# Paired block loads, weights in ten parts, and idle products in a recurrent attention and mixture-of-experts kernel

## The chip, the cores and the metric

The kernel runs on one core of a Trainium2 chip. The metric is the device time of one execution in microseconds. Before the change the median of three runs was 463.25 us (462.76 to 464.66). About 0.5% of that, 2.3 us, can be told from no change.

## The reference

Two parts follow each other. The first is a gated linear recurrence for 4 batch rows and 8 heads, 768 time steps, head size 48:

```python
for t in range(S):
    state = alpha[:, :, t, :, None] * state + np.einsum('bhd,bhe->bhde', k[:, :, t], v[:, :, t])
    y[:, :, t] = np.einsum('bhd,bhde->bhe', q[:, :, t], state)
```

Its result, seen as 3072 rows of 384 numbers, goes through a mixture of eight experts. Each row picks the expert with the largest logit:

```python
logits = x @ w_gate
expert_idx = np.argmax(logits, axis=1)
...
h = np.maximum(x_sorted[lo:hi] @ w1[e], 0.0)
y_sorted[lo:hi] = h @ w2[e]
...
return gate_w[:, None] * y
```

All data are 32-bit floats. An expert's w1 is 384 x 1024, its w2 1024 x 384.

## The kernel before

**Blocks.** Time is cut into 6 chunks of 128 steps. A block s is one chunk of one batch row with all 8 heads: chunk s // 4, batch row s % 4, so 24 blocks, chunk by chunk. Within a block the recurrence is done with matrix products; between chunks a state per batch row is carried on.

**What happens to a block.** Its parts, by the names of the functions: `load` brings alpha, k, q and v (192 KB each, in pieces of 48 numbers, 192 bytes) from memory, on the queue of SyncE. `logs` takes the logarithm of alpha on ScalarE. `cums` makes the running sum over time with a product by a triangular matrix on TensorE (tile `cum`, one PSUM bank), and its exponentials `cp` and `icp` on ScalarE. It also sends one row of each to the tiles `dec`, by small transfers on SyncE's queue. `operands` multiplies k by icp and q by cp on GpSimd, into one of three buffers `kqb`. `transposes` turns them on TensorE; ScalarE and VectorE copy the results out. `scores` multiplies them (tiles `sA`, `sB`), and `mask` applies the triangle on VectorE. `scale_state`, `read_state`, `attend` and `keys_values` read and build the state and the result `y`. `result` copies y out on ScalarE (`yT`), `rows` multiplies it by `iw`, which holds a unit matrix and the gate's weights, `logits` and `gate` work out the gate, and `keep_rows` scales the rows and writes them to a table in memory (`x_rows`).

**Decay.** A new chunk needs the decay of the state over the old one. `decay_rows(c)` makes it on VectorE in the tile `er` (lines 246 and 247) from the `dec` rows of all four blocks of chunk c, and from `alpha0`, the first alpha row of the chunk. `decay_cols(c)` then turns it on TensorE (tile `ep`, line 258), in the bank of `cum`.

**The order.** It is written out by hand: each engine runs its own instructions in the order of the program. The main loop goes over steps i from -4 to 24; step i does the scores of block i and, at fixed distances, the earlier and later parts of other blocks: `result`, `rows`, `logits`, `gate` and `keep_rows` for block i-1, `transposes` for i+1, `operands` for i+2, and running sums up to block i+5 (`sums_to`), two of them in each of steps 0, 1 and 2. `decay_rows(c)` stands in step 4c-1, `decay_cols(c)` in step 4c. `loads(i)` brings v of block i, k and q of block i+2 and the alphas that the next step's logarithms need; the loop calls it three steps ahead.

**SyncE's queue.** Its program order in a step is: block loads (`load`, line 218), the `dec` rows (line 241), then the `x_rows` of line 386, which wait for ScalarE. It issues one transfer after another, and one that waits holds those behind it. Before the loop ScalarE's queue issues two transfers for the gate's weights and five for `alpha0` (line 416), ahead of the first logarithm.

**Expert weights.** The first expert's w1 and w2 (1.5 MB each, lines 160 and 163) are loaded by `fetch` at the end of step 14. The experts' products use Strassen's scheme with seven products for eight, so sums of weight quarters are needed. `weight_sums` makes them: four of 128 x 512 for each layer, for the first expert on GpSimd, all four in one go at the end of steps 22 and 23; for later experts on VectorE.

**Afterwards** a routing stage works out which row goes to which expert, and eight groups of rows are gathered, multiplied and scattered. The change leaves these stages as they were.

Of the kernel before, what the change touches and what calls it, by code (L numbers as in the profile page):

```python
# [8 lines left out]
F32 = mybir.dt.float32  # L9
# [3 lines left out]
AF = mybir.ActivationFunctionType  # L13
# [5 lines left out]
def kernel(  # L19
# [62 lines left out]
    def first_consts():  # L82
        make_upper_triangular(nc, cmask[:], 1.0, diag=True)

        nc.vector.tensor_copy(cum_m[HC:, :], cmask[HC:, :])
        nc.vector.tensor_scalar_add(cum_m[:HC, :], cmask[:HC, :], -1.0)
        make_identity(nc, ident[:])
        for t in kqb:
            nc.vector.memset(t[:, :, :, :, D:], 0.0)

    def second_consts():
        nc.vector.tensor_scalar_mul(iw[:, :, D2:], iw[:, :, D2:], -1.0)
        for i in range(2):
            nc.vector.tensor_copy(
                iw[i * DP : (i + 1) * DP, :, i * D : (i + 1) * D],
                ident[i * DP : (i + 1) * DP, None, i * DP : i * DP + D].to_broadcast([DP, NP, D]),
            )
        nc.gpsimd.memset(er[:], 0.0)

    lt_strict = consts.tile([C, C], F32)  # L100
    ones_sq = consts.tile([C, C], F32)
# [55 lines left out]
    def fetch(ex, layer):  # L157
        if layer == 1:
            w = wpool.tile([C, DB, F], F32, name="w1")
            nc.sync.dma_start(w[:], moe_w1[bass.ds(ex, 1)].rearrange("e (a p) f -> p (e a) f", p=C))  # L160
        else:
            w = wpool.tile([C, FB, Dm], F32, name="w2")
            nc.sync.dma_start(w[:], moe_w2[bass.ds(ex, 1)].rearrange("e (a p) d -> p (e a) d", p=C))
        return w
# [8 lines left out]
    def add(eng, out, a, b):  # L173
        eng.tensor_tensor(out, a, b, op=ALU.add)  # L174

    def sub(eng, out, a, b):
        eng.tensor_tensor(out, a, b, op=ALU.subtract)  # L177

    def weight_sums(g, layer, eng):
        if layer == 1:  # L180
            t = g["s1"] = spool.tile([C, 4, HF], F32, name="s1", bufs=1)
            w1 = g["w1"]
            a11, a12, a21, a22 = [w1[:, j, i * HF : (i + 1) * HF] for i in range(2) for j in range(2)]
        else:
            t = g["s2"] = spool.tile([C, 4, FH, C], F32, name="s2")
            w2 = g["w2"]
            a11, a12, a21, a22 = [
                w2[:, j * FH : (j + 1) * FH, i * C : (i + 1) * C] for i in range(2) for j in range(2)
            ]
        add(eng, t[:, 0], a21, a22)  # L190
        sub(eng, t[:, 1], t[:, 0], a11)
        sub(eng, t[:, 2], a11, a21)
        sub(eng, t[:, 3], a12, t[:, 1])

# [6 lines left out]
    with tc.tile_pool(name="ld", bufs=6) as ld, \  # L201
         tc.tile_pool(name="work", bufs=2) as work, \
         tc.tile_pool(name="ps", bufs=1, space=PSUM) as ps, \
         tc.manual_schedule():
        st = {s: {} for s in range(NT)}
        y = ps.tile([C, 2, 512], F32, name="y")
        decay = {}

# [2 lines left out]

        kvv = y[:, :, 2 * C : 2 * C + D2].rearrange("r g (j e) -> r g j e", j=2)

        def load(s, n):
            c, b = cb(s)
            t = ld.tile([C, H, D], F32, name=n + "_sb", bufs=8 if n == "a" else 6)
            src = {"a": alpha, "k": k, "q": q, "v": v}[n]
            nc.sync.dma_start(t[:], src[b, :, c * C : (c + 1) * C, :].rearrange("h p d -> p h d"))
            st[s][n] = t

        def logs(s):
            t = work.tile([C, Dm], F32, name="lna", bufs=4)
            nc.scalar.activation(t[:], st[s]["a"][:].rearrange("s h d -> s (h d)"), AF.Ln)  # L223
            st[s]["lna"] = t

        def cums(s):
            c, b = cb(s)
            cum = ps.tile([C, 512], F32, name="cum")
            nc.tensor.matmul(cum[:, :Dm], lhsT=cum_m[:], rhs=st[s]["lna"][:], start=True, stop=True)  # L229
            cp = work.tile([C, Dm], F32, name="cp", bufs=6)  # L230
            icp = work.tile([C, Dm], F32, name="icp", bufs=6)
            nc.scalar.activation(icp[:], cum[:, :Dm], AF.Exp, scale=-1.0)
            nc.scalar.activation(cp[:], cum[:, :Dm], AF.Exp)
            st[s]["cp"], st[s]["icp"] = cp, icp


            for cc, i, row in ((c, 1, icp[0:1, :]), (c + 1, 0, cp[C - 1 :, :])):
                if 0 < cc < NB:
                    if cc not in decay:
                        decay[cc] = work.tile([B, 2, Dm], F32, name="dec", bufs=3)  # L240
                    nc.sync.dma_start(decay[cc][b : b + 1, i, :], row)

        def decay_rows(c):
            t = by_half(er[:B])
# [4 lines left out]
        def by_half(t):  # L249
            return t.rearrange("s p a d -> s a p d")[:, :, :, :D]  # L250
# [11 lines left out]
        def operands(s):  # L262
            d = st[s]
            kq = kqb[s % 3]
            for i, n, e in ((0, "k", "icp"), (1, "q", "cp")):
                nc.gpsimd.tensor_tensor(  # L266
                    by_half(kq[:, i]), d[n][:].rearrange("s (a p) d -> s a p d", a=2),
                    d[e][:].rearrange("s (a p d) -> s a p d", a=2, p=NP), op=ALU.mult,
                )

# [118 lines left out]
        def do(f, i, *a):  # L389
            if 0 <= i < NT:  # L390
                f(i, *a)
# [4 lines left out]
        def sums_to(i):  # L396
            return {-2: 0, -1: 1, 0: 3, 1: 5}.get(i, -1 if i < 0 else min(i + 5, NT - 1))

        def new_sums(i):
            return range(sums_to(i - 1) + 1, sums_to(i) + 1)  # L400

        def loads(i):
            for s in new_sums(i + 1):
                load(s, "a")
            for s, n in ((i, "v"), (i + 2, "k"), (i + 2, "q")):
                do(load, s, n)

        loads(-3)
        loads(-2)
        nc.gpsimd.memset(iw[:], 0.0)  # L410
        for i in range(2):
            nc.scalar.dma_start(
                iw[i * DP : i * DP + D, :, D2:], moe_w_gate.rearrange("(m i d) e -> i d m e", i=2, d=D)[i],
            )
        for c in range(1, NB):
            nc.scalar.dma_start(alpha0[:, c], alpha[:, :, c * C, :])
        nc.vector.memset(y[:], 0.0)
        first_consts()
        for i in range(-4, NT + 1):
            loads(i + 3)  # L420
            do(scores, i)
            do(result, i - 1)
            do(add_state, i - 1)
            for s in new_sums(i + 1):
                logs(s)
            if 0 < i < NT and i % B == 0:
                decay_cols(i // B)
            do(mask, i, 0)
            do(mask, i, 1)
            do(transposes, i + 1)  # L430
            for s in new_sums(i):
                cums(s)
            do(operands, i + 2)
            do(scale_state, i)
            if 0 < i + 1 < NT and (i + 1) % B == 0:
                decay_rows((i + 1) // B)
            do(rows, i - 1)
            do(read_state, i)
            do(attend, i)
            do(keys_values, i)  # L440
            do(logits, i - 1)
            do(gate, i - 1)
            do(keep_rows, i - 1)
            if i == -3:
                second_consts()
            late_consts(i - 1)
            if i == 14:
                groups[0]["w1"] = fetch(0, 1)
                groups[0]["w2"] = fetch(0, 2)
            if i == NT - 2:  # L450
                weight_sums(groups[0], 1, nc.gpsimd)
            if i == NT - 1:
                weight_sums(groups[0], 2, nc.gpsimd)


    sm = ctx.enter_context(tc.tile_pool(name="moe_sm", bufs=1))
# [367 lines left out]
    with tc.manual_schedule():  # L824
        weights(1, 1)
        weights(1, 2)
        gather(groups[0])
        gather(groups[1])
        turn(groups[0])
        row_sums(groups[0])  # L830
        for i, g in enumerate(groups):
            nxt = groups[i + 1] if i + 1 < E else None
            rest = []

            def begin():
                p1, tail = layer2(g)
                p1()
                rest.append(tail)

            layer1(g, rows_out(groups[i - 1]) if i else iter(()), begin)  # L840
            weights(i + 2, 1)
            if i + 2 < E:
                gather(groups[i + 2])

            def ahead():
                if nxt:
                    weight_sums(nxt, 1, nc.vector)
                    weight_sums(nxt, 2, nc.vector)

            def between():  # L850
                if nxt:
                    turn(nxt)
                    row_sums(nxt)

            rest[0](ahead, between)
            weights(i + 2, 2)
        for _ in rows_out(groups[-1]):
            pass
# [40 lines left out]
```

## Time and profile before

| | |
|---|---|
| median of 3 runs | 463.25 us (462.76 to 464.66) |
| the profiled execution | 460.42 us |
| its span, first to last instruction | 458.7 us |
| TensorE busy | 405.7 us (88%) |
| VectorE, ScalarE, GpSimd busy | 232.0, 172.4, 140.6 us |
| attention half | about 0 to 155 us |
| routing | about 155 to 183 us |
| experts | about 183 us to the end |
| DMA packets | 120162, of them 103382 under 512 B |

PE is TensorE, PEld its weight loads, DVE VectorE, ACT ScalarE, POOL GpSimd, SP SyncE; a q behind a name means the engine's queue of issues. In a timeline row the first two numbers are the start and the duration in us, then come engine, source line, operation, the tile written and the tiles read, and the number of instructions; in square brackets stands the idle time of the engine before it and what ended it. In the page's rows of digits a digit is the busy share of one of 40 equal slices, in tenths; PEclk is the granted clock of TensorE.

### The profile page before, as it was taken

To read this page: it belongs to the slowest core of one execution; us is meant where nothing else is said; L and a number is where in the kernel's file an instruction comes from. 1 tells how busy PE (TensorE), PEld (TensorE's weight loads), DVE (VectorE), ACT (ScalarE), POOL (GpSimd) and SP (SyncE) were. 2 spreads that over 40 slices of the span, in tenths; PEclk is the share of its full clock that TensorE was granted. 3 is DMA by queue.
4 is the path that set the end of the run, shared out by engine and by line. 5 is a ranking of instruction groups with operands and counts; after the bars stand their busy time and mean duration, and the time that the engine had idled before them with its cause. 6 is when DMAs were issued, how large, how long until landed. Compare 5 with 4: busy or idle time off the path is not lost.

```text
span 458.7 us, 9011 instructions
## 1 busy us (share of the span) xinstructions
PE 405.7 (88%) x3342; PEld 354.6 (77%) x3342; DVE 232.0 (51%) x639; ACT 172.4 (38%) x454; POOL 140.6 (31%) x170
## 2 busy tenths in 40 slices
PE   2888999999989514999999999999999999999991
PEld 1667888888878412988988988988988979979970
DVE  2335555555546493465366366365375473473500
ACT  3554656565533300431441441441531523513411
POOL 3425544444449236400140140140140230200102
PEclk9999999999999855999999999999999999999996
DMA  8977978889952155321523523532542452300001
GB/s 172 219 161 164 195 156 183 180 185 303 205 127 66 53 195 158 92 95 43 173 94 120 173 87 126 173 103 107 171 140 75 165 205 76 111 2 17 32 0 51
DMA packets 120162, 59.06 MB, mean 129 GB/s; under 512 B 103382, under 2 KB 114735, under 8 KB 120116
## 3 DMA queue, kind: packets, MB, share of 16 engines
q1 hardware_dynamic: 116096, 48.83, 40.6%
q0 software_dynamic: 3424, 9.59, 6.0%
q8 instruction: 27, 0.44, 0.4%
q14 instruction: 19, 0.16, 0.1%
q10 hardware_dynamic: 596, 0.04, 0.1%
HBM read 48.95 MB, written 9.58 MB: 128 GB/s over the span
## 4 chain that ended last, share of the span: by engine, by line
PE 77%; issue 8%; DMA 4%; DVE 4%; ACT 2%; POOL 2%; SPq 1%; POOLq 0%; ACTq 0%; DVEq 0%
PE pA L690 12%; PE pB L690 9%; PE pA L746 8%; PE pC L761 8%; PE sA L288 5%; PE pC L690 5%; PE y L325 5%; PE tp L276 4%; PE pB L746 4%; PE x L360 4%; PE cum L229 3%; PE pC L746 2%; PE y L315 2%; DMA w<-in_moe_w_dram 2%; PE tp L608 2%
## 5 line engine op out<-in xcount | busy, mean ns | idle before, releaser
L778 POOL DMA_INDIRECT out_dram<-zo,s_idx x29 | 31.8, 1096 | 207.0 <-ACT zo L777 145.7
L634 ACT COPY u<-pA 128x212 f32<-128x212 f32 (+7 forms) x80 | 25.5, 319 | 82.2 <-PE pA L746 77.6
L174 DVE TENSOR_TENSOR h_sb<-pB,u 128x212 f32<-128x212 f32 (+7 forms) x64 | 23.1, 361 | 64.5 <-PE pB L690 49.2
L266 POOL TENSOR_TENSOR kqb<-k_sb,icp 128x384 f32<-128x384 f32 x24 | 24.7, 1027 | 72.4 <-ACT xs L385 37.2
L761 PE MATMUL pC<-h_sb,w 128*128 128x424 f32 (+7 forms) x128 | 43.9, 496 | 0.0
L761 PEld LDWEIGHTS pC<-h_sb,w 128*128 128x128 f32 x128 | 24.1, 190 | 16.0 <-issue 6.7
L690 PE MATMUL pA<-t,s 128*128 128x212 f32 (+7 forms) x128 | 32.8, 338 | 1.0 <-ACT u L634 0.4
L598 POOL DMA_INDIRECT xg<-x_rows,g_idx x29 | 29.9, 1032 | 10.7 <-issue 7.0
L690 PE MATMUL pA<-xgT,w 128*128 128x212 f32 (+7 forms) x128 | 32.5, 335 | 0.0
L229 PE MATMUL cum<-lna,cum_m 128*128 128x384 f32 x48 | 21.4, 529 | 11.4 <-ACT lna L223 7.2
L360 PEld LDWEIGHTS x<-iw,yT 128*128 128x128 f32 x192 | 24.7, 191 | 7.3 <-ACT yT L344 2.5
L276 PE MATMUL tp<-ident,kqb 128*128 128x128 f32 x192 | 27.1, 285 | 2.4 <-POOL kqb L266 2.4
L177 DVE TENSOR_TENSOR th<-h_sb,th 128x212 f32<-128x212 f32 (+7 forms) x64 | 23.1, 361 | 10.5 <-ACT h_sb L703 10.5
L634 ACT COPY p<-pA 128x212 f32<-128x212 f32 (+7 forms) x40 | 13.2, 329 | 40.3 <-DVE t L177 25.8
L288 PE MATMUL sA<-qT,kT 48*128 48x128 f32 x192 | 27.9, 285 | 0.0
L288 PE MATMUL sB<-qT,kT 48*128 48x128 f32 x192 | 27.9, 285 | 0.0
L690 PE MATMUL pC<-xgT,w 128*128 128x212 f32 (+7 forms) x128 | 27.4, 338 | 0.0
L690 PE MATMUL pB<-t,w 128*128 128x212 f32 (+7 forms) x128 | 27.0, 333 | 0.0
L360 PE MATMUL x<-iw,yT 128*128 128x104 f32 x192 | 25.2, 274 | 2.0 <-ACT yT L344 2.0
L276 PEld LDWEIGHTS tp<-ident,kqb 128*128 128x128 f32 x192 | 21.3, 144 | 6.3 <-POOL kqb L266 4.2
L703 ACT ACTIVATE h_sb<-h_sb 128x424 f32<-128x424 f32 (+7 forms) x32 | 17.1, 533 | 24.0 <-DVE h_sb L174 24.0
L288 PEld LDWEIGHTS sA<-qT,kT 48*128 48x128 f32 x192 | 23.3, 188 | 2.7 <-issue 1.6
(174 smaller groups left out, 918.7 us busy)
## 6 DMA issues: line engine op xcount, KB each, us to landing
w<-in_moe_w_dram SPq DMA_DIRECT2D x16, 1536.0 KB, 7.6
a_sb<-in_alpha_dram SPq DMA_DIRECT2D x24, 192.0 KB, 3.3
k_sb<-in_k_dram SPq DMA_DIRECT2D x24, 192.0 KB, 3.7
q_sb<-in_q_dram SPq DMA_DIRECT2D x24, 192.0 KB, 4.2
v_sb<-in_v_dram SPq DMA_DIRECT2D x24, 192.0 KB, 3.3
x_rows<-xs SPq DMA_DIRECT2D x24, 192.0 KB, 2.2
xg<-x_rows,g_idx POOLq DMA_INDIRECT x29, 5.4
out_dram<-zo,s_idx POOLq DMA_INDIRECT x29, 2.8
```

Source lines behind the costliest of these rows:

```text
L174: eng.tensor_tensor(out, a, b, op=ALU.add)
L229: nc.tensor.matmul(cum[:, :Dm], lhsT=cum_m[:], rhs=st[s]["lna"][:], start=True, stop=True)
L266: nc.gpsimd.tensor_tensor(by_half(kq[:, i]), d[n][:].rearrange("s (a p) d -> s a p d", a=2), d[e][:].rearrange("s (a p d) -> s a p d", a=2 ...
L276: nc.tensor.transpose(tp[:, p, :], pair(kqb[s % 3][:, i], p), ident[:])
L288: nc.tensor.matmul(t[:, p, :], lhsT=d["kT"][r : r + D, p, :], rhs=d["qT"][r : r + D, p, :], start=True, stop=True,)
L360: nc.tensor.matmul(d["x"][:, m, : D2 + E], lhsT=d["yT"][:, m // 2, m % 2, :], rhs=iw[:, m, :], start=True, stop=True,)
L598: nc.gpsimd.indirect_dma_start(out=g["xg"][:r, j, :], out_offset=None, in_=x_d[:, :], in_offset=bass.IndirectOffsetOnAxis(ap=g["gi"](j, r) ...
L634: nc.scalar.copy(t[:, :m], bank["A"][:, :m])
L690: nc.tensor.matmul(out, lhsT=ops[n_][0], rhs=ops[n_][1], start=first and n_ == names[0], stop=True, skip_group_check=True,)
L746: nc.tensor.matmul(out, lhsT=lhs, rhs=rhs, start=first and f == 0, stop=True, skip_group_check=True)
L761: nc.tensor.matmul(d2[:, :n], lhsT=w2[:, f, 2 * C :], rhs=h[:, f, :n], start=(f == 0), stop=(f == FB - 1),)
L778: ins = nc.gpsimd.indirect_dma_start(out=out[:, :], out_offset=bass.IndirectOffsetOnAxis(ap=g["si"](j, r), axis=0), in_=zo[:r], in_offset= ...
```

## The change

- **Loads of two blocks.** From block 2 on, one transfer brings alpha, k, q or v of blocks s and s+1 (the same chunk, two batch rows). Counters in `loads` tell what is there already, so such transfers are issued in odd steps, four of them in the steady part, and none in even steps. The pieces stay 192 bytes. There are four double buffers for alpha and v, three for k and q.
- **Alpha rows.** The five transfers for `alpha0` move from ScalarE's queue to SyncE's, each among the `dec` rows of the first block of its chunk.
- **First weights in ten parts.** One part (256 KB for w1, 384 KB for w2) at the end of each of steps 4 to 13.
- **Idle products.** `er` is cleared by VectorE at the start, not by GpSimd. Four products of it with itself (128 x 128 by 256 columns), whose results nobody reads, stand ahead of the loop, and three more in step -1, ahead of the first transposes.
- **Second running sums apart.** Where a step makes two running sums, the second stands behind `rows`.
- **Weight sums one per step.** The eight sums for the first expert are made in steps 15 to 22, one at the end of each.

```diff
-        nc.gpsimd.memset(er[:], 0.0)
...
+    def fetch_part(g, i):
+
+        if i == 0:
+            g["w1"] = wpool.tile([C, DB, F], F32, name="w1")
+            g["w2"] = wpool.tile([C, FB, Dm], F32, name="w2")
+        if i < 6:
+            a, h = i // 2, i % 2
+            nc.sync.dma_start(g["w1"][:, a, h * F // 2 : (h + 1) * F // 2], moe_w1[0, a * C : (a + 1) * C, h * F // 2 : (h + 1) * F // 2])
+        else:
+            f = 2 * (i - 6)
+            nc.sync.dma_start(
+                g["w2"][:, f : f + 2], moe_w2[0, f * C : (f + 2) * C, :].rearrange("(a p) d -> p a d", p=C),
+            )
...
         add(eng, t[:, 0], a21, a22)
+        yield
         sub(eng, t[:, 1], t[:, 0], a11)
+        yield
...
-        def load(s, n):
+        def load(s, n, many):
             c, b = cb(s)
-            t = ld.tile([C, H, D], F32, name=n + "_sb", bufs=8 if n == "a" else 6)
-            src = {"a": alpha, "k": k, "q": q, "v": v}[n]
-            nc.sync.dma_start(t[:], src[b, :, c * C : (c + 1) * C, :].rearrange("h p d -> p h d"))
-            st[s][n] = t
+            t = ld.tile([C, 2, H, D], F32, name=n + "_sb", bufs=4 if n in "av" else 3)
+            src = {"a": alpha, "k": k, "q": q, "v": v}[n].rearrange("b h t d -> t (b h) d")
+            nc.sync.dma_start(
+                t[:, :many].rearrange("p b h d -> p (b h) d"), src[c * C : (c + 1) * C, b * H : (b + many) * H, :],
+            )
+            for i in range(many):
+                st[s + i][n] = t[:, i]
...
                     nc.sync.dma_start(decay[cc][b : b + 1, i, :], row)
+                if i and b == 0 and c:
+                    nc.sync.dma_start(alpha0[:, c], alpha[:, :, c * C, :])
...
-        def loads(i):
-            for s in new_sums(i + 1):
-                load(s, "a")
-            for s, n in ((i, "v"), (i + 2, "k"), (i + 2, "q")):
-                do(load, s, n)
+        loaded = dict(a=0, k=0, q=0, v=0)
+
+        def loads(*wanted):
+            for n, upto in wanted:
+                while loaded[n] <= min(upto, NT - 1):
+                    many = 1 if loaded[n] < 2 else 2
+                    load(loaded[n], n, many)
+                    loaded[n] += many
+
+        def loads_for(i):
+            loads(("a", sums_to(i + 1)), ("v", i), ("k", i + 2), ("q", i + 2))
+
+        def idle(n):
+
+            t = ps.tile([C, NP, C], F32, name="sA")
+            for _ in range(n):
+                nc.tensor.matmul(t[:, :2, :], lhsT=er[:, 0].rearrange("s a d -> s (a d)"), rhs=er[:, :2], start=True, stop=True)
...
+        nc.vector.memset(er[:], 0.0)
...
-        for c in range(1, NB):
-            nc.scalar.dma_start(alpha0[:, c], alpha[:, :, c * C, :])
         nc.vector.memset(y[:], 0.0)
         first_consts()
+        idle(4)
         for i in range(-4, NT + 1):
-            loads(i + 3)
+            loads_for(i + 3)
...
+            if -2 < i < 0:
+                idle(3)
             do(transposes, i + 1)
-            for s in new_sums(i):
+            sums = list(new_sums(i))
+            for s in sums[:1]:
                 cums(s)
...
             do(rows, i - 1)
+            for s in sums[1:]:
+                cums(s)
...
-            if i == 14:
-                groups[0]["w1"] = fetch(0, 1)
-                groups[0]["w2"] = fetch(0, 2)
-            if i == NT - 2:
-                weight_sums(groups[0], 1, nc.gpsimd)
-            if i == NT - 1:
-                weight_sums(groups[0], 2, nc.gpsimd)
+            if 4 <= i < 14:
+                fetch_part(groups[0], i - 4)
+            if 15 <= i < 23:
+                next(first_sums)
```

More of the change, by code (lines that the diff above doesn't have):

```diff
@@ L190, in weight_sums @@
         add(eng, t[:, 0], a21, a22)
+        yield
         sub(eng, t[:, 1], t[:, 0], a11)
+        yield
         sub(eng, t[:, 2], a11, a21)
+        yield
         sub(eng, t[:, 3], a12, t[:, 1])
+        yield
     def cb(s):
@@ L205 @@
         st = {s: {} for s in range(NT)}
+        first_sums = (None for layer in (1, 2) for _ in weight_sums(groups[0], layer, nc.gpsimd))
         y = ps.tile([C, 2, 512], F32, name="y")
@@ L212 @@
         kvv = y[:, :, 2 * C : 2 * C + D2].rearrange("r g (j e) -> r g j e", j=2)
-        def load(s, n):
+        def load(s, n, many):
             c, b = cb(s)
-            t = ld.tile([C, H, D], F32, name=n + "_sb", bufs=8 if n == "a" else 6)
-            src = {"a": alpha, "k": k, "q": q, "v": v}[n]
-            nc.sync.dma_start(t[:], src[b, :, c * C : (c + 1) * C, :].rearrange("h p d -> p h d"))
-            st[s][n] = t
+            t = ld.tile([C, 2, H, D], F32, name=n + "_sb", bufs=4 if n in "av" else 3)
[5 more added lines that the diff above has]
+                st[s + i][n] = t[:, i]
         def logs(s):
             t = work.tile([C, Dm], F32, name="lna", bufs=4)
-            nc.scalar.activation(t[:], st[s]["a"][:].rearrange("s h d -> s (h d)"), AF.Ln)
+            nc.scalar.activation(t[:], st[s]["a"].rearrange("s h d -> s (h d)"), AF.Ln)
             st[s]["lna"] = t
@@ L266, in operands @@
                 nc.gpsimd.tensor_tensor(
-                    by_half(kq[:, i]), d[n][:].rearrange("s (a p) d -> s a p d", a=2),
+                    by_half(kq[:, i]), d[n].rearrange("s (a p) d -> s a p d", a=2),
                     d[e][:].rearrange("s (a p d) -> s a p d", a=2, p=NP), op=ALU.mult,
@@ L400, in new_sums @@
             return range(sums_to(i - 1) + 1, sums_to(i) + 1)
-        def loads(i):
-            for s in new_sums(i + 1):
-                load(s, "a")
-            for s, n in ((i, "v"), (i + 2, "k"), (i + 2, "q")):
-                do(load, s, n)
-        loads(-3)
-        loads(-2)
+        loaded = dict(a=0, k=0, q=0, v=0)
[11 more added lines that the diff above has]
+                nc.tensor.matmul(t[:, :2, :], lhsT=er[:, 0].rearrange("s a d -> s (a d)"), rhs=er[:, :2], start=True, stop=True)
+        loads_for(-3)
+        loads_for(-2)
+        nc.vector.memset(er[:], 0.0)
         nc.gpsimd.memset(iw[:], 0.0)
@@ L846, in ahead @@
                 if nxt:
-                    weight_sums(nxt, 1, nc.vector)
-                    weight_sums(nxt, 2, nc.vector)
+                    for layer in (1, 2):
+                        for _ in weight_sums(nxt, layer, nc.vector):
+                            pass
             def between():
```

## The prediction

> **What bounds the kernel now.** I read the page first: where PE is not full, and at what clock.
>
> ```profile
> PE   2888999999989514999999999999999999999991
> ...
> PEclk9999999999999855999999999999999999999996
> DMA  8977978889952155321523523532542452300001
> ```
>
> A slice is 11.5 us. The attention half is slices 0 to 13. PE is full from about 48 to 128 us; there only work taken from PE would count, and the change takes none. It has thin places at the start, at 40 to 48 us, at 132 to 140 us, and in the routing at 155 to 183 us, which the change leaves alone. Second view, the timeline of the start:
>
> ```profile
> 2.25 4.35 ACTq L416 DMA_DIRECT2D alpha<-in_alpha_dram  x5
> 6.65 0.94 ACT L223 ACTIVATE lna<-a_sb 128x384 f32<-128x384 f32 x2 [4.57 <-DMA alpha<-in_alpha_dram]
> 7.23 1.65 PE L229 MATMUL cum<-lna,cum_m 128*128 128x384 f32 x2 [7.23 <-ACT lna L223]
> ...
> 17.01 0.81 PE L229 MATMUL cum<-lna,cum_m 128*128 128x384 f32 x2
> ...
> 18.79 0.91 PE L229 MATMUL cum<-lna,cum_m 128*128 128x384 f32 x2 [0.96 <-ACT cp L233]
> ```
>
> The first logarithm starts when ACT's queue has issued five small alpha loads (2.25 + 4.35 = 6.60). The first running sum takes 1.65 us, the same product later 0.81: PE began at half speed. The last row is a second running sum in one step; it waits 0.96 for the first one's bank. Third, SP's own timeline, and the chain that ended last in order of time, for the two late thin places:
>
> ```profile
> 35.26 0.89 SPq L241 DMA_DIRECT2D dec<-icp  x1
> 36.25 1.13 SPq L241 DMA_DIRECT2D dec<-cp  x1
> 37.48 0.54 SPq L241 DMA_DIRECT2D dec<-icp  x1
> ...
> 106.05 0.53 SPq L163 DMA_DIRECT2D w<-in_moe_w_dram  x1
> 106.68 2.46 SPq L218 DMA_DIRECT2D v_sb<-in_v_dram  x1
> 109.24 4.57 SPq L218 DMA_DIRECT2D k_sb<-in_k_dram  x1
> 113.90 3.38 SPq L218 DMA_DIRECT2D q_sb<-in_q_dram  x1
> ...
> 129.83 0.72 SPq L241 DMA_DIRECT2D dec<-icp  x1
> ```
>
> ```profile
> 37.48 2.15 DMA dec<-icp
> ...
> 40.42 1.23 DVE er L247
> 41.80 0.63 PE ep L258 x4
> ...
> 132.85 0.56 DVE er L246
> ```
>
> Both times a decay row is issued late. The icp row of block 7 was ready at 33.2 (its exponential starts at 32.73 and takes 0.49) and left SP at 37.48; block 23's was ready at 125.6 and left at 129.83. The first came behind a row of loads, the second behind the two 1.5 MB weight loads, after which three block loads took 10.4 us to issue, not 2. DVE stands at L246 until the row lands, and behind it on DVE are logits, gate and state, on ACT yT, on PE the decay columns.
>
> I time a step by its first score product in the timeline: steps 0 to 5 start at 13.81, 21.00, 27.87, 34.80, 39.81 and 48.25; an undisturbed step is 5.59, with decay columns 6.02. Step 4 took 8.44 and step 20 took 7.20.
>
> **The start.** Five alpha issues leave ACT's queue. The second alpha block, issued at 1.31, lands after about 3.5 (median of the first 30 us) at 4.8, so the logarithms move from 6.65 to about 4.5. The idle products need er cleared by DVE (about 0.5 from 1.1, half of y's 0.91 for 1024 columns) and run from 1.65. One has 256 columns against 384: 256/384 of 1.65 is 1.1 us at half speed, or 0.85 where they overlap; four end at 5.1 to 6.0. Thus the first sum starts at 5.1 to 6.0, not 7.23: 1.2 to 2.1 us, I take 1.7. Full speed saves 0.8 in the first sum, 0.5 in the first four transposes and up to 0.7 in the second sum; the three idle products before the transposes run while POOL makes the operands (2 us) and cost 0 if warm, 0.7 if cold. As it is not known when the clock rises, I take 1.3 of 2.0. Lead at step 0: 3.0 (bounds 1.2 and 4.1). Clearing er on DVE puts y's clearing and the triangle's copies 0.5 later, to 3.5, before the first sum wants them; on POOL it saves nothing.
>
> **Second running sums apart.** In step 0 there are no rows to slip in: 0. In steps 1 and 2 the eight row products (0.87 in the chain) fill the waits of 0.96 and 1.02: 0.87 each, 1.7. Lead at step 3: 4.7. Scores of block 4 would end at 39.81 + 1.1 - 4.7 = 36.2.
>
> **Loads of two blocks.** The DMA view of 0 to 30 us shows 30045 packets on the SP queue's ring and 98% of the 16 engines: the start is bound by packets of 192 B, and a double load has twice as many. What matters is when the icp row of block 7 leaves. In both programs 34 block loads stand ahead of it (12 alpha, 6 v, 8 k, 8 q). The 26th was issued by 23.97 before; packets being the bound, it stays there. Before, small issues followed between loads, 37.48 in all. Now: three dec rows at 0.63 (29.14 to 31.79 has four in 2.6) end at 25.9; then four double loads, eight blocks, which in the full stretch from 9.79 to 16.50 took 6.7, end at 32.6; then eight small issues (dec rows, one alpha row moved here, x rows), 5.0, and block 7's row leaves at 37.6. Change: +0.1. Bounds: the eight blocks at an unhindered 0.5 each (44.57 has 0.42, 45.83 has 0.53) give 34.9, -2.6; one more stall as at 56.87 (2.16 for a 0.7 issue) gives +1.5. I take +0.1, since the ring is full there. So the lead of 4.7 ends in a wait at step 4. The reader of the first of two blocks now waits for both, 0.85 longer (8 loads in 6.7). The tightest is q of block 2: the eleventh load landed at 13.25 (v, issued at 9.79, median 3.5), the fifteenth then at 16.7, POOL's product ends at 17.7, and its transposes come at about 19: cost 0, and 0.85 without that cover, which the wait at step 4 swallows too. L247 took 1.23 beside a POOL product and 0.55 in its median; POOL will have finished, so -0.7. The decay columns come at 41.2, and PE stands from 36.2 to 41.2, 5 us.
>
> **The clock after that wait.** The page shows half clock after PE went idle at 155. The windows give a mean of 0.76 for 180 to 190, so 4.8 us of it at half and full speed from 184.8, 6.3 us after work came back at 178.5; at the start it took from 7.23 to about 14, where score products fall from 0.52 to 0.27. If a 5 us wait drops the clock, it stays low to somewhere between 44 and 48. Up to 43.9 DVE's and ACT's chain (logits, gate, yT, state: 2.9 us from er to the next sum) hides it; behind that, half of the low time is lost: 0 to 2.1, I take 1.0. Step 4 in all: 0.1 - 0.7 + 1.0 = +0.4.
>
> The Trainium skill, "TensorE: Matmul & The Clock Gate", Part 1, has the clock rise after a busy window of about 3.4 us and fall after an idle one. That speaks for the four idle products and against this change's waiting 5 us at step 4; by it the loss there would be up to 1.7, and the sum 0.7 higher. The same skill, "DMA: Bandwidth & Descriptors", Rules for kernel authors, says to coalesce small transfers into large ones. Here the 192 B pieces stay as they are, so I give it nothing; by the rule the lead of 4.7 would be kept.
>
> **Weights in ten parts.** Ten issues of about 0.53 in steps 4 to 13, against the two before; SP has then four double loads, four dec rows, two x rows and two parts in two steps: 6.7 + 2.6 + 1.3 + 1.1 = 11.7 against 11.2 of PE. It slips 0.5 per two steps, 2.5 in all. A chunk's last dec row comes about 9.1 after its group of loads began and lands 2.5 later; with 1.1 for er that is 12.7, and PE wants it 17.9 after the group's step begins: 5 us of cover. If that goes, a chunk costs 2.2. Cost 0. Gain: block 23's row leaves at about 126 and lands by 129, before DVE gets to L246 (130.85). Step 20 becomes 4.60 (step 21) plus 0.43 for decay columns, 5.03: -2.2.
>
> **Weight sums one per step.** Eight of 1.27 us leave POOL's run from 141.1 to 151.7. Nobody waits there: the state of block 23 was ready at 146.7 and wanted at 151.25. Gain 0. In steps 15 to 22 each stands behind the scaled state (done 124.84) and ahead of the next operands, which cannot start before 127.98: 3.1 us for 1.27, cost 0; without that cover 1.27 a step, 10 in all.
>
> **Sum.** +0.4 - 2.2 = -1.8. The profiled execution took 460.42 (span 458.7 and 1.7 around it), so 458.6; the median of the runs is 463.25, 2.8 above the profiled one, so 461.4.
>
> **Rivals.** (1) The lead survives in part. If loads issue unhindered, block 7's row leaves 2.6 earlier, PE waits little over 2 us, the clock holds: -2.6 - 0.7 - 2.2 = -5.5, 457.7. For it: SP has fewer issues; against it: 98% of the engines. Chance 0.25. (2) The idle products do not raise the clock in time. The lead is then 1.2 + 1.7 = 2.9, the wait at step 4 is 3.2 and may leave the clock up: 0.1 - 0.7 - 2.2 = -2.8, 460.4. Chance 0.15. (3) Slower: the groups of eight blocks, with weight parts among them, put SP more than 5 us late, and the decay rows of the next chunks hold DVE as block 7's does. Price 2.2 for each of three chunks, and step 20's gain lost: 0.4 + 6.6 = +7.0, 470.2; with one chunk late, +0.4. For it: 11.7 against 11.2 per two steps; against it: the cover of 5. Chance 0.15.
>
> **How the numbers follow.** My forecast has 0.45; its own range is 459.6 to 463.2, from the clock's 0 to 2.1 and one stall. A measurement of this kernel can tell about 0.5%, 2.3 us, from no change: below 460.9 is faster. That takes rival 1 (0.25), two thirds of rival 2 (0.10) and a quarter of the forecast (0.11): 0.46. Slower than 465.6: most of rival 3, and what I overlook, 0.14. The rest, 0.40, is the same. The range 457.6 to 464.6 leaves out rival 3's worse part and the far end of rival 1.
>
> **What would show it.** Right: scores of block 0 near 10.8, of block 3 near 30; PE idle some 5 us in step 4 before decay columns at about 41, low clock after; step 20 near 5.0; no load issue over 3 us at 106. Wrong: block 7's icp row leaving before 36, steps 8, 12 or 16 over 6.5, or step 20 still at 7.

## The result and the profile after

The changed kernel takes 474.36 us (median of four runs, 473.43 to 474.73) against 463.0 of the kernel before beside it: a ratio of 1.0236, interval 1.0206 to 1.0267. It is slower. The predicted time was 461.4, the range 457.6 to 464.6; what was called rival 3 is what happened.

The page of the profiled execution (474.5 us, span 472.7) shows where. First the slices, now 11.8 us each:

```profile
PE   7893979979799921699999999999999999999991
...
PEclk9997998979999965599999999999999999999997
DMA  9986788989862107414235225315414432400001
```

The start is fuller than before (7 8 against 2 8). In place of one thin slice at 40 to 48 us there are four, 3, 7, 7 and 7, two or three slices apart: one for each chunk that begins in steps 4, 8, 12 and 16. The granted clock is at half in or behind the first three (39.5 to 46.3, 70.2 to 73.6 and 97.5 to 104.3 us), and full at the fourth. The waits from 30 to 132 us (total, number of times, longest) and the two first of them in VectorE's timeline:

```profile
DVE er L269 <- DMA dec<-icp: 20.0, 4, 8.7
...
PE ep L281 <- DVE lgn L393: 13.6, 4, 7.4
```

```profile
41.47 0.55 DVE L269 TENSOR_TENSOR er<-dec 4x384 f32<-4x384 f32 x1 [8.70 <-DMA dec<-icp]
...
68.69 0.55 DVE L269 TENSOR_TENSOR er<-dec 4x384 f32<-4x384 f32 x1 [4.81 <-DMA dec<-icp]
```

L269 is what L246 was. VectorE stands there for the last icp row of a chunk, all four times, 20 us in all; TensorE then stands at the decay columns (L281), which are made from `er`; the list names L393, VectorE's next instruction behind `er`, as what ended that.

Start of the first score product of a block, and length of the steps (from TensorE's timeline), in us:

| | before | after |
|---|---|---|
| scores of block 0, block 4 | 13.81, 39.81 | 10.18, 34.17 |
| steps 0, 1, 2 | 7.18, 6.88, 6.93 | 6.89, 6.02, 6.07 |
| step 4 | 8.44 | 15.47 |
| steps 8, 12, 16 | 6.02, 6.02, 6.02 | 10.47, 11.78, 9.55 |
| step 20 | 7.20 | 5.19 |
| scores of block 23 | 149.09 | 162.18 |

The other steps are the same in both (5.0 in step 3, then 5.59, 4.94, 4.6). The balance: a lead of 5.64 at block 4, then +7.03, +4.45, +5.76 and +3.53 in steps 4, 8, 12 and 16, and -2.01 in step 20: 13.1 us behind at block 23, of 14.0 in the span. From there to the first expert product it is 33.2 us in both, so the other 0.9 comes in the experts; the half clock around the routing lasted 30.7 us and not 27.3, and no run takes that apart.

Why the rows come late is seen on SyncE's queue. Its issues in the changed kernel around the second wait, from behind the last of four double loads to the next group:

```profile
61.26 1.57 SPq L262 DMA_DIRECT2D dec<-icp  x1
62.92 0.53 SPq L262 DMA_DIRECT2D dec<-cp  x1
63.55 0.53 SPq L409 DMA_DIRECT2D x_rows<-xs  x1
64.13 0.42 SPq L185 DMA_DIRECT2D w<-in_moe_w_dram  x1
64.65 0.50 SPq L262 DMA_DIRECT2D dec<-icp  x1
...
67.42 0.44 SPq L236 DMA_DIRECT2D a_sb<-in_alpha_dram  x1
67.96 1.89 SPq L236 DMA_DIRECT2D v_sb<-in_v_dram  x1
```

The row that VectorE awaits until 68.67 leaves at 64.65, directly behind a weight part that lands at 68.49. From one group of loads to the next (54.05, 67.42, 81.11, 94.34, 107.94, 121.50) the queue needs 13.2 to 13.7 us for two steps, and TensorE at its own pace 11.2 to 11.6. Before, nine steps took it 50.4 us (49.62 to 99.99), 5.6 each: TensorE's pace. So SyncE falls some 2 us per two steps behind, TensorE stands at each chunk until the queue has caught up, and that is the time of the kernel up to step 16.

### The profile page after: what moved, and what is told of

Same layout as the page of the kernel before. It is cut to its first block, busy times and chain, and to the rows that moved or that the text cites. A ratio compares the mean times of both kernels' runs of the same rounds, so it can differ in the third digit from the quotient of the medians.

```text
span 472.7 us, 8960 instructions
## 1 busy us (share of the span) xinstructions
PE 415.8 (88%) x3356; PEld 362.7 (77%) x3356; DVE 233.3 (49%) x640; ACT 171.8 (36%) x454; POOL 139.6 (30%) x169
## 4 chain that ended last, share of the span: by engine, by line
PE 58%; issue 5%; DVE 4%; POOL 2%; ACT 1%; DMA 1%; POOLq 0%; ACTq 0%; DVEq 0%
PE pA L727 12%; PE pB L727 9%; PE pA L783 8%; PE pC L798 8%; PE pC L727 5%; PE pB L783 4%; PE pC L783 2%; PE tp L645 2%; PE sA L311 2%; PE y L348 1%; PE x L383 1%; PE tp L828 1%; PE tp L299 1%; PE y L338 1%; DVE xgT L646 1%
## 5 line engine op out<-in xcount | busy, mean ns | idle before, releaser
L727 PE MATMUL pA<-t,s 128*128 128x212 f32 (+7 forms) x128 | 33.2, 341 | 1.0 <-ACT u L671 0.4
L299 PE MATMUL tp<-ident,kqb 128*128 128x128 f32 x192 | 28.6, 294 | 1.3 <-POOL kqb L289 1.3
L671 ACT COPY p<-pA 128x212 f32<-128x212 f32 (+7 forms) x40 | 13.1, 328 | 40.4 <-DVE t L176 25.8
L299 PEld LDWEIGHTS tp<-ident,kqb 128*128 128x128 f32 x192 | 22.7, 149 | 4.4 <-POOL kqb L289 2.3
L289 POOL TENSOR_TENSOR kqb<-q_sb,cp 128x384 f32<-128x384 f32 x24 | 24.9, 1035 | 2.3 <-DMA q_sb<-in_q_dram 2.3
```

The costliest lines, as they stand in the source:

```text
L289: nc.gpsimd.tensor_tensor(by_half(kq[:, i]), d[n].rearrange("s (a p) d -> s a p d", a=2), d[e][:].rearrange("s (a p d) -> s a p d", a=2, p ...
L299: nc.tensor.transpose(tp[:, p, :], pair(kqb[s % 3][:, i], p), ident[:])
L671: nc.scalar.copy(t[:, :m], bank["A"][:, :m])
L727: nc.tensor.matmul(out, lhsT=ops[n_][0], rhs=ops[n_][1], start=first and n_ == names[0], stop=True, skip_group_check=True,)
```

## The experiments

Each kernel is an edit of the changed kernel or of the one before; ratios are to the kernel before, with their 95% intervals. "Queue" means the time between two groups of block loads on SyncE's queue. Steps and queue are from one profile each.

**Which part of the change does it?** *singles*: the change with one block per load.

```diff
-                    many = 1 if loaded[n] < 2 else 2
+                    many = 1
-            t = ld.tile([C, 2, H, D], F32, name=n + "_sb", bufs=4 if n in "av" else 3)
+            t = ld.tile([C, 1, H, D], F32, name=n + "_sb", bufs=8 if n == "a" else 6)
```

> The change with one block per load again (all else as changed). Theory Q: in the double loads SyncE's queue takes 13.5 us per two steps against 11.2 of PE, as eight blocks go out in a row and the small decay rows stand behind them; with single loads the small issues run while packets drain, so steps 8, 12 and 16 come down from 10.5, 11.8 and 9.6 to about 6.0, step 20 stays at 5.2, step 4 stays about 14 (34 loads still stand ahead of block 7's row): about 461 us. Theory P (the ten weight parts hold the queue, not the double loads): steps 8 and 12 stay over 8, 468 to 472.

473.21 us, 1.0241 (1.0208 to 1.0275): no different from the change. Steps 4, 8, 12 and 16 take 16.07, 12.07, 6.32 and 12.99, the queue some 6.6 a step (55.05 to 94.85 us). The double loads are not the cause. *pairs_only* confirms it from the other side: the kernel before with `load` and `loads` of the change and nothing else.

> The kernel before with the double loads alone. Theory Q: without parts the queue needs about 11.5 us per two steps: some lateness at step 4 (block 7's row leaves at 38 to 40, not 37.5) and little after; 464 to 467. Theory P: 463, no change.

462.41, 1.0016 (0.9997 to 1.0036). Steps 8, 12 and 16 stay at 6.02; step 4 is 9.49, and step 18, where the weights now stand between two groups, 7.67.

*whole*: the change with both weights loaded whole at the end of step 14, and the sums in steps 22 and 23.

```diff
-            if 4 <= i < 14:
-                fetch_part(groups[0], i - 4)
-            if 15 <= i < 23:
-                next(first_sums)
+            if i == 14:
+                groups[0]["w1"] = fetch(0, 1)
+                groups[0]["w2"] = fetch(0, 2)
+            if NT - 2 <= i < NT:
+                for _ in range(4):
+                    next(first_sums)
```

> The change with the first weights whole at the end of step 14 and the sums in steps 22 and 23 again (double loads and all else as changed). Theory P: steps 8 and 12 fall to about 6.0, step 20 goes back to about 7: 464 us. Theory Q: the parts are 1.0 us of issue and about 2 us of transfer of the 13.5 per two steps, so part of the lateness stays: steps 8 and 12 about 7 to 9, 467 to 470.

467.22, 1.0118 (1.0082 to 1.0153): half of the loss goes with the parts. Step 8 is back at 6.02, step 12 takes 6.84, but step 4 still 14.82 and step 16 8.39, and step 18 takes 9.47 behind the two large loads. *before_parts* adds only the ten parts and the sums one per step to the kernel before.

> The kernel before with the ten weight parts and the one-per-step sums alone (single loads, no idle products, nothing else). If the parts by themselves overload SyncE's queue: a step of that queue grows from 5.6 to about 6.6 us, steps 8, 12 and 16 go over 7 and step 20 falls to 5.0: 468 to 472. If it needs the double loads or the alpha rows beside them: 461, as step 20's 2.2 us are won and nothing is lost.

471.31, 1.0138 (1.0070 to 1.0207). Steps 8, 12 and 16 go from 6.02 to 7.17, 12.15 and 9.82, step 20 from 7.20 to 5.19, the queue to 6.7 a step on average (46.34 to 112.96 us; 5.7 to 7.5 singly): the parts alone put it behind.

*alpha_back*: the change with the five alpha rows on ScalarE's queue again, ahead of the loop, as before.

> The change with the five alpha rows issued by ScalarE's queue ahead of the loop again. Each is 0.8 us of SyncE's queue, one per chunk: without them steps 8, 12 and 16 lose about 0.8 each, against a start later by 1 to 2 us that step 4 swallows: 471 to 473. If the rows were not in the way: 474.

470.39, 1.0120 (1.0050 to 1.0191); scores of block 0 at 11.88, step 4 13.81, step 8 8.28, steps 12 and 16 9.95 and 10.44. With the alpha rows off SyncE's queue some 4 of the 11 us are gone. And *before_alpha_sp*, the kernel before with only these five transfers moved among the `dec` rows:

```diff
-        for c in range(1, NB):
-            nc.scalar.dma_start(alpha0[:, c], alpha[:, :, c * C, :])
...
                     nc.sync.dma_start(decay[cc][b : b + 1, i, :], row)
+                if i and b == 0 and c:
+                    nc.sync.dma_start(alpha0[:, c], alpha[:, :, c * C, :])
```

> The kernel before with the five alpha rows alone moved from ScalarE's queue to their places on SyncE's. If SyncE's queue has no room in steps 4 to 16, 0.8 us a chunk counts in full: +2.4 to +4, 464.5 to 466.5, while the logarithms start 2 us earlier and step 4 swallows that. If the queue has room: 461 to 462.5.

470.09, 1.0131 (1.0077 to 1.0185). The start gains its 3 us (block 0 at 10.83), and yet the kernel loses: step 4 takes 13.14, because block 7's icp row leaves even later than before, at 40.17:

```profile
38.78 0.66 SPq L241 DMA_DIRECT2D dec<-icp  x1
39.54 0.54 SPq L241 DMA_DIRECT2D dec<-cp  x1
40.17 0.54 SPq L241 DMA_DIRECT2D dec<-icp  x1
```

Steps 8 and 12 take 6.25 and 6.98, and step 20 11.78. The direction was expected, the size was not; five transfers of 0.7 to 0.8 us don't add up to it. In step 20 block 23's icp row left at 135.48, 5.65 later than before, while the step began only 3.93 later, and the clock was at half from 142.3 to 149.1; why the queue was that late there stays open.

*start_only*: the change with single loads, whole weights and the sums in steps 22 and 23, so that only the start, the alpha rows and the second sums apart are left of it.

> The change with single loads, whole weights at step 14 and the sums in steps 22 and 23: what is left is the start (idle products, er cleared by VectorE, alpha rows on SyncE's queue) and the second sums apart. Theory Q: the lead of 4 to 5 us is lost at step 4, which waits for block 7's row on SyncE's queue; alpha rows cost up to 0.8 a chunk; step 20 stays near 7: 463 to 466. If the lead could be kept without touching the decay rows' queue: 458.

467.78, 1.0152 (1.0096 to 1.0208): block 0 at 9.92, steps 4, 8 and 12 at 15.39, 7.01 and 8.28, step 20 at 7.21. That is some 2 us above what was expected: without parts and double loads the lead is still lost at step 4, and steps 8 and 12 are late as well.

**Issue time or transfer time?** *parts_act*: the parts are issued by ScalarE's queue.

```diff
     def fetch_part(g, i):
-            nc.sync.dma_start(g["w1"]...
+            nc.scalar.dma_start(g["w1"]...
```

> The change with the ten weight parts issued by ScalarE's queue, decay rows still on SyncE's. If the parts cost by their place in SyncE's order (issue theory): the queue needs 11.7 us per two steps as with whole weights, steps 8, 12, 16 near 6.0, 6.8, 8.4, no late stall: about 463 to 465. If they cost by the transfer engines' time (engine theory): steps 8 to 16 stay over 9, 470 to 475.

471.28, 1.0150 (1.0082 to 1.0217), and the queue is hardly quicker, 12.3 to 14 per two steps (steps 4, 8, 12, 16: 14.94, 11.87, 7.03, 9.55). SyncE no longer issues the parts, but its loads still share the engines with their bytes. *dec_act*: the 40 `dec` rows and the five alpha rows are issued by ScalarE's queue, right where ScalarE has made the rows.

```diff
-                    nc.sync.dma_start(decay[cc][b : b + 1, i, :], row)
+                    nc.scalar.dma_start(decay[cc][b : b + 1, i, :], row)
...
-                    nc.sync.dma_start(alpha0[:, c], alpha[:, :, c * C, :])
+                    nc.scalar.dma_start(alpha0[:, c], alpha[:, :, c * C, :])
```

> The change with the decay rows and the five alpha rows issued by ScalarE's queue (all else as changed, double loads and parts too). Theory Q: the rows no longer stand behind loads; all chunk steps 4, 8, 12, 16 come to 6.0, the lead of 5.6 us at step 4 is kept: 453 us. Theory D (the DMA engines themselves are too full, rows land late whoever issues them): steps 8 to 16 stay over 8, 468 to 473. Theory C (the clock's drops are the main loss): they come only after waits, so it follows the waits.

454.65, 0.9843 (0.9811 to 0.9874), with all parts and double loads in place. Steps 4, 8, 12, 16 and 20 take 7.06, 6.02, 6.32, 6.02 and 5.03; the queue 9.7 to 12.5 per two steps. Block 7's icp row, which left SyncE at 39.72 in the change, now leaves ScalarE at 30.31, and VectorE makes `er` at 35.50 without a wait:

```profile
30.31 0.53 ACTq L262 DMA_DIRECT2D dec<-icp  x1
```

```profile
35.50 0.54 DVE L269 TENSOR_TENSOR er<-dec 4x384 f32<-4x384 f32 x1
```

*before_dec_act* does the same to the kernel before (its `dec` rows only).

> The kernel before with the decay rows alone moved to ScalarE's queue. If lateness of these rows is what steps 4 and 20 pay: both fall to 6.0 and 5.0, -2.4 and -2.2, 457 us. If ScalarE's added issues (0.5 us each, two a step) hold the exponentials and copies: steps grow by up to 1 us, 463 or more.

457.11, 0.9846 (0.9782 to 0.9911): step 4 falls from 8.44 to 6.39, step 20 from 7.20 to 5.02. So the place of the rows in SyncE's queue already cost the kernel before its two late thin places, and it decides what the change is worth. The move takes the rows out from behind the loads and 45 issues off SyncE at once; no run separates these two.

**Later parts.** *late_parts*: the parts in steps 13 to 22, behind most chunks, the sums in steps 22 and 23.

> The change with the same ten parts on the same queue, but in steps 13 to 22, where no alpha blocks are loaded any more (sums in steps 22 and 23 again). Theory E (the transfer engines are full in steps 4 to 13 and the parts' transfer time does not fit there; since the parts issued by ScalarE cost nearly the same): steps 8 and 12 as with whole weights, 6.0 and 6.8, step 16 below 8.4, no stall at step 18 and step 20 near 5: 462 to 464. Theory I (each part costs by its issue and by cutting the queue wherever it is): steps 16 and 20 go over 8: 468 or more.

467.89, 1.0132 (1.0086 to 1.0179), some 4 us above what was hoped: steps 8 and 12 are good (6.02, 6.68), but step 4 (15.0) and step 16 (9.55) stay, and a new wait comes, for the last part, on GpSimd:

```profile
158.35 1.26 POOL L173 TENSOR_TENSOR s<-w 128x512 f32<-128x512 f32 x1 [9.43 <-DMA w<-in_moe_w_dram]
```

Block 23's scores start at 151.95, 10 us ahead of the change, and some 4 of these are lost again behind that wait. *dec_act_late* is both edits together.

> The change with decay and alpha rows on ScalarE's queue and the ten parts in steps 13 to 22. Theory E: the small delays that the parts still make with these rows moved (step 12, 6.3) and the late landing of loads go: steps 4 to 16 at 6.0 but for the start: 453.5 to 454.7. If the later parts meet the x rows and the last loads: steps 17 to 20 over 5.6, 455 or more.

457.57, 0.9907 (0.9876 to 0.9937): the steps are those of dec_act, block 23's scores start at 141.95 against 142.03, and the late last part costs 3 us. Early parts are right once the rows are out of the queue.

**Idle products and the clock.** *dec_act_noidle*: dec_act without its seven idle products.

> The change with decay and alpha rows on ScalarE's queue and without the seven idle products. They give full speed for the first sum, transposes and second sum: by the same products before, 1.3 to 2.0 us later at step 0, and that should now reach the end: 456 to 457. If the start is bound by packets behind step 0: 454.7, no difference.

455.21, 0.9863 (0.9823 to 0.9903), against 454.65 with them: no difference can be told. The clock rises at 12.4 us, not 7.7, and the products at the start run at half speed, but block 0's scores start at 10.72 in place of 10.73, and block 4's at 36.28 in place of 35.99.

*fill* asks whether the low clock behind the waits is what costs. It is the change with products of the unit matrix with itself ahead of the decay columns, 28 in step 4, 10 in steps 8 to 20.

```diff
+            for _ in range(28 if c == 1 else 10):
+                nc.tensor.matmul(ep[:, 0, :], lhsT=ident[:], rhs=ident[:], start=True, stop=True)
             for p in range(NP):
                 nc.tensor.transpose(ep[:, p, :], pair(er[:], p), ident[:])
```

> The change with products of the unit matrix on TensorE (28 in step 4, 10 in steps 8 to 20; results overwritten) ahead of each chunk's decay columns, so that it is busy while it waits. Theory C (clock): the granted clock stays full to the routing and step 4 falls by 0.4, step 12 by 2: 470 to 472. Theory Q: SyncE's queue sets the pace, what is won in one chunk is waited for in the next: 473.5 to 474.5.

475.88, 1.0278 (1.0243 to 1.0313). The clock now stays full until 173 us, and nothing is gained:

```profile
PEclk9999999999999975599999999999999999999997
```

```profile
DVE er L269 <- DMA dec<-icp: 24.9, 4, 8.5
```

The waits grow from 20.0 to 24.9 us; steps 4, 8, 12 and 16 take 14.93, 10.64, 11.18 and 10.40, in sum 47.2 against 47.3. Step 20, which has no wait to hide the added products, goes from 5.19 to 7.30. The clock is not the cause; what TensorE wins by it, it waits for the queue.

**A version that beats both.** *best*: single loads, `dec` and alpha rows on ScalarE's queue, the rest as in the change. *best2*: the same with the alpha rows left on SyncE's.

> The change with single loads and with decay and alpha rows on ScalarE's queue. Single loads let k and q of block 4 land earlier (step 2 then 6.0 and not 7.4): 453. If the queue's order no longer matters: 454.7 as with double loads.

> As best, with the five alpha rows left on SyncE's queue. If ScalarE's alpha issue (1.24 us in step 1) was on the path: 0.5 to 1 below best, 452.3; if SyncE's queue is again too full: above best, 455 or more.

best takes 455.31, 0.9841 (0.9806 to 0.9876); best2 takes **453.9, 0.9810 (0.9778 to 0.9842)**, 9.1 us less than the kernel before it and some 20 less than the change. In best2 block 0's scores start at 10.25 and block 4's at 34.39, a lead of 5.42 over the kernel before; step 4 takes 7.06 (-1.38), steps 8, 12 and 16 6.02, step 20 5.03 (-2.17): 8.97 in all at block 23. Against best, step 2 takes 6.26 and not 7.45. The waits for rows are gone from the list, and the slices show no thin place before the routing:

```profile
PE   7899999999998018899999999999999999999991
...
DMA  8999899999821174031350451451452353200001
```

## Why the prediction was wrong, point by point

**The step that failed** is the one on the weights: "SP has then four double loads, four dec rows, two x rows and two parts in two steps: 6.7 + 2.6 + 1.3 + 1.1 = 11.7 against 11.2 of PE. It slips 0.5 per two steps [...] 5 us of cover [...] Cost 0." Measured: 13.2 to 13.7. In the five cycles from 54.05 to 121.50 the four double loads took 6.0 to 7.6, 6.8 on average, much as priced; the term that was mis-sized is the small issues, 5.0 in the sum and 6.0 to 7.7 measured, 6.7 on average. The sum gave them their unhindered 0.5 to 0.65 each and left the alpha row out. The longest of them, from 73.43 to 81.11:

```profile
73.43 1.61 SPq L262 DMA_DIRECT2D dec<-icp  x1
75.10 0.73 SPq L264 DMA_DIRECT2D alpha<-in_alpha_dram  x1
75.94 0.54 SPq L262 DMA_DIRECT2D dec<-cp  x1
...
77.16 0.41 SPq L185 DMA_DIRECT2D w<-in_moe_w_dram  x1
77.67 1.66 SPq L262 DMA_DIRECT2D dec<-icp  x1
```

The first row behind the loads takes 1.61 here and 1.48 to 3.05 in the five cycles, three times the price used or more. The row directly behind a weight part takes 1.66 here, but 0.50 or 0.51 in the other four cycles. The part itself is issued in 0.41, and its transfer was not in the sum. The slip was then divided among the chunks as if each started with the full 5 us of cover; but behind the wait at step 4 the queue was late already (the loads of step 5 begin at 54.05, the step itself at 49.63), and a slip of 2 us per two steps makes 4 per chunk: steps 8, 12 and 16 lost 4.45, 5.76 and 3.53, and not the 2.2 of rival 3, whose mechanism this is. It stood at 0.15, because its cover was compared with a slip of 0.5.

**What the profile before could have told.** The queue's own pace there was 5.6 a step, TensorE's pace; a queue that keeps up that exactly has no room that is known. In windows of steady steps (last two columns: share of the DMA engines, GB/s), the kernel before and the change:

```profile
54.00:66.00 12.00, 12.00 (x180) 10.52 (x180) 6.69 (x18) 7.43 (x18) 5.68 (x7) 1.00 0.86 180
66.00:78.00 12.00, 12.00 (x175) 10.45 (x172) 6.41 (x19) 7.25 (x17) 5.28 (x8) 1.00 0.78 165
```

```profile
54.00:68.00 14.00, 13.55 (x212) 11.86 (x210) 5.43 (x14) 6.74 (x16) 6.31 (x8) 1.00 0.83 194
...
81.00:95.00 14.00, 13.78 (x220) 12.01 (x212) 5.83 (x15) 6.88 (x16) 6.05 (x8) 1.00 0.91 194
```

Eight block loads (8 x 192 KB), two x rows (2 x 192 KB) and two parts (2 x 256 KB) in 11.2 us want 222 GB/s. Without parts it is 176; the kernel before moved 165 to 180, at 0.78 to 0.86 of the engines. The changed kernel gets 194 (180 in the stretch between, 68 to 81), best2 in the same windows 213 to 224:

```profile
54.00:68.00 14.00, 14.00 (x190) 12.18 (x192) 8.61 (x24) 8.11 (x20) 6.19 (x8) 1.00 0.94 213
...
81.00:95.00 14.00, 14.00 (x198) 12.30 (x195) 7.31 (x21) 8.73 (x20) 7.08 (x9) 1.00 0.96 224
```

So the engines can carry more than they did behind the one queue. The DMA view in 40 slices of 0.2 us, the change from 73 to 81 and best2 from 56 to 64 us:

```profile
DMA  9999999999999999600000489748991353110000
```

```profile
DMA  9999999999956589532006999999999999999984
```

In the change the engines are full for 3.2 us while the backlog of the loads drains, then empty from 76.4 to 77.4 and nearly so from 79 to 81, while SyncE works through `dec`, `x_rows` and parts one by one. Full and empty alternate: what SyncE takes for small issues isn't spent on loads, and the loads hold the small ones up. In best2 there is one dip of less than a microsecond. This reading fits parts_act (the bytes cost, even from another queue) and dec_act (45 issues fewer on SyncE let the same bytes through). How the 13.5 us divide between issue and transfer can be read in part from two runs. whole, with no part in this stretch, takes 11.7 per two steps (52.66 to 99.46), which is what the prediction had for the queue with the parts; parts_act, with the parts' bytes but not their issues on SyncE, takes 13.2 (53.11 to 119.18). So most of what the parts add seems to come with their bytes. As whole runs close to TensorE's pace, its queue may need less than 11.7, so this is a reading and not a proof.

**Right: the lead, and how it is lost.** Scores of block 0 came at 10.18 for 10.8, of block 3 at 29.16 for about 30; each second sum apart gave 0.86 for 0.87. The lead ended in a wait at step 4, as told, with the low clock behind it. But its two terms don't add as they were added, 1.7 and 1.3. The alpha issues off ScalarE's queue alone give 2.98 at block 0 (before_alpha_sp, 10.83). The rest of the start, idle products among it, gives 1.93 with these issues left where they were (alpha_back, 11.88), and both together 3.63. With the issues gone, the idle products by themselves are worth 0.0 at block 0 and 0.3 at block 4 (dec_act against dec_act_noidle). Block 0 came at 9.92 to 10.72 in kernels with the start of the change (one profile each, start_only and singles the ends), so less than 0.8 isn't told apart there. Rival 1 fell at step 4's wait, rival 2 at the clock, which rose at 5.4 us.

**Mis-sized: block 7's row.** Forecast at 37.6, it left at 39.72. The four double loads ahead of it took 6.2, less than the 6.7 of the sum; again it was the small issues: three rows took 3.4 from 23.60 (1.9 in the sum), and eight issues 6.35 from 33.37 (5.0 in the sum), the first row 1.57 and the alpha row 0.82. The columns came at 42.74 for 41.2, and TensorE waited 7.41 and not 5:

```profile
42.74 1.09 PE L281 MATMUL ep<-ident,er 128*128 128x128 f32 x4 [7.41 <-DVE lgn L393]
```

In every kernel of this study that leaves the `dec` rows in SyncE's queue, block 5's scores start between 48.2 and 50.8, whether block 0's start at 9.9 or at 13.8: what is gained at the start cannot pass this point. With the rows on ScalarE's queue they start at 41.45 to 46.11.

**The clock.** From the end of `er` to the next block's scores the kernel before took 6.6 us, the change 7.0, 7.1, 8.9 and 6.7 in steps 4, 8, 12 and 16: 0.1 to 2.3 a time, 3.3 in all; the term of 1.0 at step 4 was 0.4. The Trainium skill, "TensorE: Matmul & The Clock Gate", Part 1, has the clock fall after an idle window of about 3.4 us; the half clock at 39.5 to 46.3 us, after TensorE had gone idle at 35.3 (42.74 - 7.41), agrees. But the clock also fell at 70.2 and 97.5, where TensorE had stood for only 2.41 and 1.88 us before the decay columns, and stayed up in step 16 after 1.87: here a wait shorter than that window could be enough. fill shows that the fall only adds to a wait which something else sets.

**Right: step 20, L270, the sums, the double loads.** Step 20 took 5.19 for 5.03. L270 (L247 before) took 0.55 at step 4, not 1.23. With the sums on GpSimd the steps from 17 on are as short as before, step 20 apart, and singles and pairs_only (1.0016) show neither gain nor loss from two transfers of 192 KB made into one, as the prediction had it.

## What to carry to other kernels

Before putting transfers on a queue, add up that queue's cycle with every issue at the price it has behind a full load, and compare it with the pace of the engine that bounds; a queue that only just keeps that pace may have no cover that repeats, and then a slip comes back at each point where the engine waits for it. Put the small transfers that somebody waits for on another queue than the bulk loads, at the place where their data are made. A gain ahead of such a point is only a longer wait at it, so clear the point first: the same change is worth -7 us (dec_act) or +11, depending on where 45 small rows are issued.

## What the runs showed of the hardware

- A row of 1.5 KB takes 0.50 to 0.57 us to issue on ScalarE's queue in best2 (39 of 40 rows), and 1.48 to 3.05 as the first behind a group of double loads on SyncE's queue (the change, 54 to 122 us).
- The Trainium skill, "DMA: Bandwidth & Descriptors", section "Issuing engines are not separate DMA queues", says that starting transfers on several engines "will only save the time on the sequencer it takes to initiate the DMA, which is usually small relative to the DMA itself". Here the gain was not small: 40 rows issued by ScalarE in place of SyncE gave 0.9846 on the kernel before, and with the five alpha rows 474.36 to 454.65 us on the change. How much of that is sequencer time and how much is the rows' place in the order, no run shows.
- From 54 to 95 us the engines carried 180 to 194 GB/s when SyncE's queue issued loads, parts and rows alike (the change), and 232 to 235 when ScalarE's issued the `dec` and alpha rows (dec_act, some steps further on at the same time):

```profile
54.00:68.00 14.00, 14.00 (x207) 12.37 (x202) 7.78 (x23) 8.52 (x20) 6.86 (x9) 1.00 0.93 232
```
